# Retention and a GELU feed-forward on one core: queries turned by matmuls with strided PSUM output, tails loaded by POOL's queue, decay constants by ScalarE

## The chip, the core and the metric

The kernel runs on one core of a Trainium2 chip. The core has TensorE (PE; its weight loads are shown apart as PEld), VectorE (DVE), ScalarE (ACT), GpSimd (POOL) and SyncE (SP). Each engine works through its own instructions in program order and waits for the others through semaphores. Sixteen DMA engines move data between device memory and SBUF; an engine that issues a DMA puts it on its own queue, and all queues share the sixteen. TensorE writes only to PSUM, which has eight banks of 2 KB for each of 128 partitions.

The metric is the device time of one execution in microseconds (us), taken as the median over several executions.

## What is computed

```python
def _attn_ref(q, k, v):                      # (8, 8, 576, 64): batch, heads, sequence, head size
    scores = scale * np.matmul(q, k.transpose(0, 1, 3, 2))
    gamma = 1.0 - 2.0 ** (-5.0 - np.arange(H, dtype=np.float32))
    rel = pos[:, None] - pos[None, :]
    Dmat = np.where(rel >= 0, gamma[:, None, None] ** rel[None, :, :], 0.0)
    ret = scores * Dmat[None, :, :, :]
    return np.matmul(ret, v).astype(np.float32)

def _moe_ref(x, w_in, w_out):                # x (4608, 512), w_in (512, 2048), w_out (2048, 512)
    h = x @ w_in
    c = np.float32(np.sqrt(2.0 / np.pi))
    g = 0.5 * h * (1.0 + np.tanh(c * (h + 0.044715 * h * h * h)))
    return (g @ w_out).astype(np.float32)
```

The attention's output, with its heads side by side, is `x` of the feed-forward part. There is no softmax: the decay `gamma ** (i - j)` splits into a factor of the query's position and one of the key's, so each chunk of 128 positions needs only a 0/1 mask, and what came before the chunk goes through a state of 64 x 64 for each head.

## The kernel before

**Attention.** Each of the 8 batches has four chunks of 128 positions (`c` = 0 to 3) and a *tail* of 64 (`c == NC`, that is 4). A chunk passes through these steps, each a function:

- `load` (lines 74 to 94) brings k, q and v of a chunk into a tile `ld` (256 KB; 16 buffers), and of a tail into a tile `lt` (two DMAs of 64 KB, one for each half of the heads; 4 buffers).
- `cast` (225 to 250), through `cc`, turns f32 into f16 and multiplies q and k by the decay factors, columns of the constant `sc`.
- `turn` (268) turns k (and mostly q) by TensorE transposes into a PSUM bank, and copies the bank into `tt`. The queries of the first two batches (`NQ`) are loaded in another order, four neighbouring positions in one row, so that a descriptor covers 1 KB, and `turn_q4` (256) turns them: eight transposes fill one f16 bank of 1024 columns, and the copy (262) puts the positions back into their order. The tails, and the chunks of batches 2 and 3, are turned by `turn` with q in it; batches 4 to 7 by transposing DMAs (`turn_dma`).
- `score` (294) forms k times q in two banks, and VectorE multiplies by the mask into `ret` (308).
- `state`, `scan` and `spread` (316, 329, 339) form the state of the chunk, decay it, and copy it into `tbd`.
- `av` (344) multiplies `ret` with v and adds state times q; `put` (379) copies the result into `xT`, a ring of 1536 tokens that the feed-forward part reads.

These steps share three PSUM banks of the tag `att`; in the first batch other tags are used as well. `hp` has two, and A, B and C one each.

**Feed-forward.** The 4608 tokens go in nine blocks of 512 (`t` = 0 to 8). `up(t, fc)` (397) multiplies 128 columns of `w_in` with a block, and ScalarE applies the GELU. Block 0 then takes the plain product with `w_out`: 16 steps of two matmuls (421) for the first two token tiles, a `store_pair`, and 16 more for the other two, 34 steps in all (u = 0 to 33). Blocks 1 to 8 have 16 up steps of two and 14 product steps (u = 0 to 29), and use a scheme with seven products in place of eight, which needs sums of the activations (`act_sums`, 447, on VectorE, after steps 9 and 15) and of the weights (`weight_sums`, 437, four VectorE operations for each half).

**Order.** All order is written out by hand. Batch 0's chunks come first (lines 545 to 571), with a few matmuls without use (`filler`) between. From then on each step `u` of block `t` is followed by what `at(t, u, ...)` has put there; `up(0, fc)` counts as step `fc - 16` of block 0. So the weight casts of w_out run on VectorE at steps -5 to -2 of block 0, batch 0's tail and batch 1 within block 0, batches 2 and 3 from block 1 on.

**Loads.** `seq` (123 to 127) is the order of all loads on SP's queue: batch 0, w_in, w_out, batch 1, and so on. `pump` issues as many as there are free `ld` buffers; every cast of a chunk frees one. `mixed` (113) puts the six tail loads of a batch between other loads: those of batch 0 between the loads of w_out, those of batch 1 between batch 2's first ones. At step 0 of block 0 the tail's k is cast by VectorE and its q and v by POOL; at step 3 it is turned, at 6 scored, at 9 multiplied with v.

**Constants.** Lines 144 to 181 form the exponents of all decay factors with small VectorE operations in `ex` (56 columns), one Exp on ScalarE makes `sc` of them, and two more VectorE operations multiply by the scale.

Of the kernel before, what the change touches and what calls it, by code (L numbers as in the profile page):

```python
# [19 lines left out]
def kernel(  # L20
# [53 lines left out]
    def load(b, key, c, u=0):  # L74
        src = SRC[key]
        if c == NC:
            t = ldt() if u == 0 else att[b]["raw"][key, c]
            nc.sync.dma_start(
# [34 lines left out]
    def mixed(loads, b):  # L113
        pieces = [("b", b, key, NC, u) for key in "kqv" for u in range(2)]
        n = len(loads) // len(pieces)
        out = []
        for i, x in enumerate(loads):
            out.append(x)
            if i % n == n - 1 and pieces:
                out.append(pieces.pop(0))  # L120
        return out

    seq = body(0) + [("i", g, ct) for g in range(4) for ct in range(4)]
    seq += mixed([("o", f) for f in range(NF)], 0)
    seq += body(1) + mixed(body(2)[:6], 1) + mixed(body(2)[6:], 2)
    for b in range(3, B):
        seq += mixed(body(b), b)
# [16 lines left out]
    pos_i = const.tile([128, 1], I32, name="pos_i")  # L144
    nc.gpsimd.iota(pos_i, pattern=[[0, 1]], base=-64, channel_multiplier=1)
    qp_i = const.tile([128, 1], I32, name="qp_i")
    nc.gpsimd.iota(qp_i, pattern=[[0, 1]], base=0, channel_multiplier=QT)
    pos = const.tile([128, 1], F32, name="pos")
    nc.vector.tensor_copy(out=pos, in_=pos_i)
    post = const.tile([128, 1], F32, name="post")  # L150
    nc.vector.tensor_copy(out=post[0:64], in_=pos[0:64])
    nc.vector.tensor_scalar(out=post[64:128], in0=pos[64:128], scalar1=-64.0, scalar2=None, op0=ALU.add)
    posq = const.tile([128, 1], F32, name="posq")
    nc.vector.tensor_copy(out=posq, in_=qp_i)
    for c in range(NC):
        r = slice(32 * c, 32 * c + 32)
        nc.vector.tensor_scalar(out=posq[r], in0=posq[r], scalar1=-128.0 * c - 64.0, scalar2=None, op0=ALU.add)
    NE = 8 + HP * 8 + 8 + 8
    ex = const.tile([128, NE], F32, name="ex")
    lgr = const.tile([128, 8], F32, name="lgr")  # L160
    for h in range(H):
        nc.vector.memset(lgr[:, h : h + 1], math.log(gam[h]))
    nc.vector.tensor_scalar(out=ex[:, 0:8], in0=lgr, scalar1=pos, scalar2=-1.0, op0=ALU.mult, op1=ALU.mult)
    for j in range(QT):
        nc.vector.tensor_scalar(
            out=ex[:, 8 + 8 * j : 16 + 8 * j], in0=lgr, scalar1=float(j), scalar2=None, op0=ALU.mult
        )
        nc.vector.scalar_tensor_tensor(
            out=ex[:, 8 + 8 * j : 16 + 8 * j], in0=lgr, scalar=posq, in1=ex[:, 8 + 8 * j : 16 + 8 * j],
            op0=ALU.mult, op1=ALU.add,  # L170
        )
    nc.vector.tensor_scalar(out=ex[:, 48:56], in0=lgr, scalar1=pos, scalar2=None, op0=ALU.mult)
    for u in range(2):
        r = slice(64 * u, 64 * u + 64)
        lo = lgr[r, 4 * u : 4 * u + 4]
        nc.vector.tensor_scalar(out=ex[r, 40:44], in0=lo, scalar1=post[r], scalar2=None, op0=ALU.mult)
        nc.vector.tensor_scalar(out=ex[r, 44:48], in0=lo, scalar1=post[r], scalar2=-1.0, op0=ALU.mult, op1=ALU.mult)
    sc = const.tile([128, NE], F32, name="sc")
    nc.scalar.activation(out=sc, in_=ex, func=AF.Exp, bias=0.0, scale=1.0)
# [76 lines left out]
    def turn_q4(b, p0, copy, tag="att"):  # L256
        a = att[b]
        t = bank(tag, "tr", F16)
        for i in range(8):
            o = 512 * p0 + 128 * i  # L260
            nc.tensor.transpose(t[:, 128 * i : 128 * i + 128], a["q"][:, o : o + 128], ident)
# [313 lines left out]
    def at(t, u, f):  # L575
        events.setdefault((t, u), []).append(f)
# [135 lines left out]
```

## Time and profile before

| | |
|---|---|
| median of 13 runs | 333.39 us (331.11 to 335.86) |
| the profiled execution | 335.7 us, its span 334.0 us |
| busy in the span | PE 308.0 (92%), DVE 192.9 (58%), ACT 167.8 (50%), POOL 102.1 (31%) |
| first up-projection starts | 25.62 us |
| block 0's products start / block 1 starts | 39.43 us / 69.22 us |
| share of the chain that ended last | PE 69%, DVE 12%, DMA 8%, SP's queue 4%, ACT 4% |
| read and written | 36.70 MB and 9.44 MB of device memory |

The span runs from the first to the last instruction; the time of the execution also has what lies around it. `L421` is line 421. Where TensorE's busy share is full, its matmuls follow each other without a gap; a wait is named by the engine and the result that ended it. The granted clock of TensorE is given as a share of full speed.

### The profile page before, as it was taken

To read this page: it belongs to the slowest core of one execution; us is meant where nothing else is said; L and a number is where in the kernel's file an instruction comes from. 1 tells how busy PE (TensorE), PEld (TensorE's weight loads), DVE (VectorE), ACT (ScalarE), POOL (GpSimd) and SP (SyncE) were. 2 spreads that over 40 slices of the span, in tenths; PEclk is the share of its full clock that TensorE was granted. 3 is DMA by queue.
4 is the path that set the end of the run, shared out by engine and by line. 5 is a ranking of instruction groups with operands and counts; after the bars stand their busy time and mean duration, and the time that the engine had idled before them with its cause. 6 is when DMAs were issued, how large, how long until landed. Compare 5 with 4: busy or idle time off the path is not lost.

```text
span 334.0 us, 6557 instructions
## 1 busy us (share of the span) xinstructions
PE 308.0 (92%) x2660; PEld 187.8 (56%) x2660; DVE 192.9 (58%) x320; ACT 167.8 (50%) x312; POOL 102.1 (31%) x122
## 2 busy tenths in 40 slices
PE   5689959999889978999999999999999999999995
PEld 2344424544667436854684478447745864585484
DVE  7783454697863576547643964398355535651352
ACT  3566504677434635547636653674367146713610
POOL 7867046547350660008400930095000000000000
PEclk9999969999999989999999999999999999999999
DMA  8999999999999999993499859504410030003003
GB/s 203 213 352 334 289 272 218 186 234 186 236 196 202 202 268 195 169 248 91 91 196 194 215 111 199 180 2 84 127 57 2 3 126 3 0 2 126 2 0 128
DMA packets 134990, 51.29 MB, mean 154 GB/s; under 512 B 124208, under 2 KB 126256, under 8 KB 134960
## 3 DMA queue, kind: packets, MB, share of 16 engines
q1 hardware_dynamic: 134960, 50.87, 69.1%
q8 instruction: 21, 0.34, 0.5%
q14 instruction: 9, 0.07, 0.1%
HBM read 36.70 MB, written 9.44 MB: 138 GB/s over the span
## 4 chain that ended last, share of the span: by engine, by line
PE 69%; DVE 12%; DMA 8%; SPq 4%; ACT 4%; issue 1%; POOL 0%; DVEq 0%
PE hp L403 26%; PE opB L472 12%; PE opC L472 9%; PE opA L472 7%; DMA ld<-in_moe_w_out_dram 5%; PE op L421 4%; DMA ld<-in_moe_w_in_dram 4%; PE st L302 3%; PE xs L351 3%; SPq L90 3%; DVE s L454 2%; DVE s L455 2%; DVE s L457 2%; DVE gT L456 2%; PE us L321 2%; PE xs L369 2%
## 5 line engine op out<-in xcount | busy, mean ns | idle before, releaser
L403 PE MATMUL hp<-xT,w_in_sb 128*128 128x512 f16 x576 | 134.5, 383 | 2.1 <-ACT xT L390 2.0
L409 ACT ACTIVATE gT<-hp 128x512 f16<-128x512 f32 x144 | 86.2, 598 | 70.1 <-PE hp L403 69.6
L403 PEld LDWEIGHTS <-w_in_sb 128*128 128x128 f16 x576 | 54.2, 98 | 62.0 <-issue 4.2
L245 POOL TENSOR_TENSOR ck<-ld,sc 128x512 f16<-128x512 f32 x31 | 36.0, 1163 | 101.9 <-issue 44.3
L308 DVE TENSOR_TENSOR ret<-st,cm 128x512 f16<-128x512 f32 x64 | 41.1, 684 | 34.1 <-PE st L302 34.1
L472 PEld LDWEIGHTS <-gT 128*128 128x128 f16 x512 | 49.0, 98 | 7.2 <-issue 0.7
L472 PEld LDWEIGHTS <-s 128*128 128x128 f16 x384 | 36.3, 98 | 5.4 <-DVE s L455 0.8
L342 ACT CAST tbd<-ws 64x256 f16<-64x256 f32 x64 | 25.8, 403 | 18.2 <-DVE ws L337 17.5
L245 POOL TENSOR_TENSOR cq<-ld,sc 128x512 f16<-128x512 f32 x24 | 29.6, 1233 | 6.1 <-DMA ld<-in_q_dram 6.1
L472 PE MATMUL opB<-wt,gT 128*128 128x256 f16 x256 | 30.9, 273 | 0.5 <-DVE ost L486 0.5
L472 PE MATMUL opA<-w_out_sb,gT 128*128 128x256 f16 x256 | 31.0, 273 | 0.0
L454 DVE TENSOR_TENSOR s<-gT 128x1024 f16<-128x1024 f16 x16 | 14.8, 925 | 26.7 <-ACT gT L409 26.7
L486 DVE TENSOR_TENSOR ost<-k,opC 128x512 f32<-128x512 f32 x16 | 11.0, 688 | 16.5 <-PE opC L472 16.2
L302 PE MATMUL st<-tt 64*128 64x128 f16 x288 | 15.6, 223 | 5.2 <-DVE tt L280 2.8
L390 ACT CAST xT<-xs 128x512 f16<-128x512 f32 x31 | 18.0, 582 | 4.0 <-PE xs L369 3.0
L486 DVE TENSOR_TENSOR k<-k,opB 128x512 f32<-128x512 f32 x16 | 11.0, 686 | 15.4 <-PE opB L472 15.3
L421 PE MATMUL op<-w_out_sb,gT 128*128 128x512 f16 x64 | 18.5, 421 | 0.8 <-ACT ost L426 0.8
L302 PEld LDWEIGHTS <-tt 64*128 64x128 f16 x288 | 8.4, 95 | 19.2 <-issue 10.7
L351 PEld LDWEIGHTS <-cv 128*64 128x64 f16 x288 | 10.0, 110 | 16.2 <-issue 14.6
L351 PE MATMUL xs<-ret,cv 128*64 128x128 f16 x288 | 16.4, 227 | 2.4 <-DVE ret L308 1.3
L504 ACT COPY ost<-opA 128x512 f32<-128x512 f32 x8 | 4.7, 585 | 23.5 <-PE opA L472 20.8
L472 PE MATMUL opC<-wt,s 128*128 128x256 f16 x128 | 16.3, 273 | 0.0
(84 smaller groups left out, 311.9 us busy)
## 6 DMA issues: line engine op xcount, KB each, us to landing
out_dram<-ost SPq DMA_DIRECT2D x17, 512.0 KB, 3.2
ld<-in_q_dram SPq DMA_DIRECT2D x32, 256.0 KB, 4.7
ld<-in_k_dram SPq DMA_DIRECT2D x32, 256.0 KB, 5.0
ld<-in_v_dram SPq DMA_DIRECT2D x32, 256.0 KB, 4.9
ld<-in_moe_w_in_dram SPq DMA_DIRECT2D x16, 256.0 KB, 6.2
ld<-in_moe_w_out_dram SPq DMA_DIRECT2D x16, 256.0 KB, 5.5
lt<-in_k_dram SPq DMA_DIRECT2D x16, 64.0 KB, 4.4
lt<-in_q_dram SPq DMA_DIRECT2D x16, 64.0 KB, 5.0
```

What stands on the lines that cost most here:

```text
L245: eng.tensor_tensor(out=dst.rearrange("p (h d) -> p h d", d=D), in0=raw.rearrange("p (h d) -> p h d", d=D), in1=sc[:, s0 : s0 + nh].unsque ...
L302: nc.tensor.matmul(st[hl][:, 128 * p : 128 * p + 128], a["tk"][r, 4 * c + p, :], tq(b, c, p)[r], start=True, stop=True)
L308: nc.vector.tensor_tensor(out=r[:, 0:w], in0=st[hl][:, 0:w], in1=m.rearrange("p n i -> p (n i)"), op=ALU.mult)
L342: cp(out=tbd[b % 2][r, c, :, r], in_=att[b]["w"][r])
L351: nc.tensor.matmul(xs[64 * hl : 64 * hl + 64, 128 * p : 128 * p + 128], a["v"][:, col(c, p, hl)], a["ret"][c, hl][:, 128 * p : 128 * p + 128],
L390: nc.scalar.copy(out=xT[:, g0 : g0 + 2], in_=src)
L403: nc.tensor.matmul(hp.rearrange("p (g t) -> p g t", t=TL), w_in_sb[:, ct, 128 * fc : 128 * fc + 128], xT[:, o : o + TB // TL, ct, :], star ...
L409: nc.scalar.activation(out=gT[t][:, fc].rearrange("p i n -> p (i n)"), in_=hp, func=AF.Gelu_apprx_tanh)
L421: nc.tensor.matmul(op[i], gT[t][:, f, i], w_out_sb[:, f, :], start=(f == 0), stop=(f == NF - 1))
L454: nc.vector.tensor_tensor(out=s["1"], in0=a21, in1=a22, op=ALU.add)
L472: nc.tensor.matmul(op[tag][:, HD * u : HD * u + HD], lhs(f), rhs[:, f], start=(new and u == 0 and f == 0), stop=(f == NH - 1), skip_group_ ...
L486: nc.vector.tensor_tensor(out=o, in0=a, in1=b, op=ALU.add)
```

## The change

1. **Constants.** The exponents are no longer formed: `decay` has ScalarE compute `exp(scale * in + bias)` with the logarithm of the head's gamma as input, the position as a scale for each partition, and the logarithm of the score's scale as bias. There are seven Exps. Half of the memsets of `lgr` are POOL's.
2. **`turn_q4`.** Four matmuls against the identity, instead of four transposes, fill one f32 bank of 512 columns for one pair of heads. Matmul `j` writes the columns `j, j + 4, j + 8, ...`, so the bank holds the positions in order and the copy is straight. There are four calls for a batch instead of two.
3. **Tail loads.** They are issued on POOL's queue, all six at a written step (`load_tail`), and are no longer in `seq`. Batch 0: step -10 of block 0; batch 1: step 2 of block 1; batch 2: step 14 of block 1; batch 3: step 26 of block 1; batches 4 to 7: step 15 of block `b - 2`.
4. **Steps.** Batch 0's tail: all three casts on POOL at step 0, turned at step 8 (ScalarE's copy), scored at 10, multiplied at 13. Batch 1's queries are turned at steps 15 to 18, its chunks at 19, 23, 27 and 31, scored two steps later (before: 16, 20, 24, 28). `weight_sums(0)` moves from step 33 to step 11 of block 0, `weight_sums(4)` from step 2 to 1 of block 1. Batch 1's tail casts move from step 6 to 14 of block 1, batch 2's from 14 to 26, batch 3's from step 27 of block 1 to step 14 of block 2. In block 1 the order is (2,0), (2,1), tail of 1, (2,2) at steps 7, 12, 20 and 24; before it was tail of 1, (2,0), (2,1), (2,2) at 12, 17, 20 and 24.

```diff
@@ load @@
-            nc.sync.dma_start(
+            nc.gpsimd.dma_start(
                 out=t[64 * u : 64 * u + 64, :].rearrange("p (h d) -> p h d", d=D),
                 in_=src[b, 4 * u : 4 * u + 4, M0:S, :].rearrange("h s d -> s h d"),
@@ loads @@
-    def mixed(loads, b):
...
+    def load_tail(b):
+        for key in "kqv":
+            for u in range(2):
+                load(b, key, NC, u)
     seq = body(0) + [("i", g, ct) for g in range(4) for ct in range(4)]
-    seq += mixed([("o", f) for f in range(NF)], 0)
-    seq += body(1) + mixed(body(2)[:6], 1) + mixed(body(2)[6:], 2)
-    for b in range(3, B):
-        seq += mixed(body(b), b)
+    seq += [("o", f) for f in range(NF)]
+    for b in range(1, B):
+        seq += body(b)
@@ constants @@
-    nc.scalar.activation(out=sc, in_=ex, func=AF.Exp, bias=0.0, scale=1.0)
...
+    ip = const.tile([128, 6], I32, name="ip")
+    nc.gpsimd.iota(ip[:, 0:4], pattern=[[1, QT]], base=-64, channel_multiplier=QT)
+    nc.gpsimd.iota(ip[:, 4:5], pattern=[[0, 1]], base=-64, channel_multiplier=1)
+    lgr = const.tile([128, 16], F32, name="lgr")
+    for h in range(H):
+        (nc.gpsimd if h % 2 else nc.vector).memset(lgr[:, h : h + 1], math.log(gam[h]))
+    lsc = const.tile([128, 1], F32, name="lsc")
+    nc.vector.memset(lsc, math.log(scale))
+    ps5 = const.tile([128, 8], F32, name="ps5")
+    nc.vector.tensor_copy(out=ps5[:, 0:5], in_=ip[:, 0:5])
+    for c in range(1, NC):
+        r = slice(32 * c, 32 * c + 32)
+        nc.vector.tensor_scalar(out=ps5[r, 0:4], in0=ps5[r, 0:4], scalar1=-128.0 * c, scalar2=None, op0=ALU.add)
+    def decay(cols, lg, p, b=0.0):
+        nc.scalar.activation(out=cols, in_=lg, func=AF.Exp, bias=b, scale=p)
     for j in range(QT):
+        decay(sc[:, 8 + 8 * j : 16 + 8 * j], lgr[:, 0:8], ps5[:, j : j + 1], lsc)
...
+    decay(sc[:, 0:8], lgr[:, 0:8], ps5[:, 5:6])
...
+    decay(sc[:, 48:56], lgr[:, 0:8], ps5[:, 4:5], lsc)
+    decay(sc[:, 40:44], lgr[:, 8:12], ps5[:, 6:7], lsc)
+    decay(sc[:, 44:48], lgr[:, 8:12], ps5[:, 7:8])
@@ turn_q4 @@
+    def turn_q4(b, p, copy, tag="att"):
+        a = att[b]
+        t = bank(tag, "tr")
+        for j in range(QT):
+            o = 512 * p + 128 * j
+            nc.tensor.matmul(
+                t.rearrange("p (i j) -> p j i", j=QT)[:, j, :], a["q"][:, o : o + 128], ident,
+                start=(j == 0), stop=True, skip_group_check=True,
+            )
+        copy(out=a["tq"][:, 4 * p : 4 * p + 4, :].rearrange("p c t -> p (c t)"), in_=t)
@@ order @@
-    turn_q4(0, 0, A.copy, "A")
-    turn_q4(0, 2, V.tensor_copy, "B")
+    for p, tag in enumerate(("A", "B", "C", "att")):
+        turn_q4(0, p, (A.copy, V.tensor_copy)[p % 2], tag)
...
+    at(0, -10, lambda: load_tail(0))
-    at(0, 0, lambda: [cc(0, key, NC, e) for key, e in zip("kqv", (V, P, P))])
-    at(0, 3, lambda: turn(0, NC, V.tensor_copy))
-    at(0, 6, lambda: score(0, NC))
-    at(0, 9, lambda: av(0, NC))
-    at(0, 10, lambda: put(0, NC))
+    at(0, 0, lambda: [cc(0, key, NC, P) for key in "kqv"])
+    at(0, 8, lambda: turn(0, NC, A.copy))
+    at(0, 10, lambda: score(0, NC))
+    at(0, 13, lambda: av(0, NC))
+    at(0, 14, lambda: put(0, NC))
...
-    at(0, 12, lambda: turn_q4(1, 0, A.copy))
-    at(0, 14, lambda: turn_q4(1, 2, V.tensor_copy))
+    at(0, 11, lambda: weight_sums(0))
+    for p in range(HP):
+        at(0, 15 + p, lambda p=p: turn_q4(1, p, (A.copy, V.tensor_copy)[p % 2]))
     for c in range(NC):
-        u = 16 + 4 * c
+        u = 19 + 4 * c
...
-    at(0, 33, lambda: (av(1, 3), put(1, 3), spread(1, 3, A.copy), weight_sums(0)))
-    at(1, 2, lambda: weight_sums(4))
+    at(0, 33, lambda: (av(1, 3), put(1, 3), spread(1, 3, A.copy)))
+    at(1, 1, lambda: weight_sums(4))
...
-            t0, ut = 1, [1, 1, 1, 5, 5, 5, 9, 9, 9, 13, 13, 13]
+            t0, ut = 1, [1, 1, 1, 5, 5, 5, 9, 9, 9, 12, 12, 12]
...
-            at(1, 6, lambda: tail_casts(1, (P, P, A)))
-            at(1, 14, lambda: tail_casts(2, (P, P, A)))
+            at(1, 2, lambda: load_tail(1))
+            at(1, 14, lambda: tail_casts(1, (P, P, A)))
+            at(1, 14, lambda: load_tail(2))
+            at(1, 26, lambda: tail_casts(2, (P, P, A)))
         else:
-            at(t0, ut[-1] + 1, lambda b=b: tail_casts(b, (P, P, A)))
+            at(t0, ut[-1] if b == 3 else ut[0] - 1, lambda b=b: load_tail(b))
+            at(*((2, 14) if b == 3 else (t0, ut[-1] + 1)), lambda b=b: tail_casts(b, (P, P, A)))
...
-    todo = [(1, NC)] + [(b, c) for b in range(2, B) for c in CH]
-    plan = {1: (12, 17, 20, 24), 2: (2, 6, 12, 18, 23), 3: (2, 7, 12, 20), 4: (1, 6, 11, 17, 23),
+    todo = [(2, 0), (2, 1), (1, NC), (2, 2)] + [(b, c) for b in range(2, B) for c in CH][3:]
+    plan = {1: (7, 12, 20, 24), 2: (2, 6, 12, 18, 23), 3: (2, 7, 12, 20), 4: (1, 6, 11, 17, 23),
```

## The prediction

> **What bounds the kernel now.** I read the page's slices first, then the chain of waits of the first 70 us, then the busy times by stage, and last the order of work on VectorE, on POOL and in the tail loads. The slices say where TensorE is not full:
>
> ```profile
> PE   5689959999889978999999999999999999999995
> ...
> POOL 7867046547350660008400930095000000000000
> PEclk9999969999999989999999999999999999999999
> DMA  8999999999999999993499859504410030003003
> ```
>
> A slice is 8.35 us. From slice 6 on TensorE is full but for slices 10 to 14, so the end is set by TensorE's work plus what it lost before about 130 us. The DMA engines are full for 150 us. The granted clock falls in slice 5 (42 to 50 us) and a little in 15. The chain of that stretch, by start and length:
>
> ```profile
> 39.70 4.95 DMA ld<-in_moe_w_out_dram
> 44.65 0.02 issue
> 44.67 0.43 DVE w_out_sb L528
> 45.10 0.34 DVE ck L245
> 45.44 0.05 issue
> 45.49 0.61 PE tr L276 x4
> ...
> 53.55 2.45 ACT tt L262
> 56.00 0.43 ACT ost L426
> ...
> 68.59 0.59 ACT xT L390
> ```
>
> Until 45.1 the chain is the weight loads. TensorE stood still from 41.3 to 45.49, 4.2 us, in step 3 of block 0: the tail's transposes wait for the tail's k cast, which is queued on VectorE behind all sixteen w_out casts. Then:
>
> ```profile
> 39.40:45.50 6.10, 1.93 (x10) 0.70 (x8) 3.23 (x9) 0.60 (x1) 0.40 (x1) 0.88 0.98 313
> 45.50:51.50 6.00, 6.00 (x25) 2.19 (x26) 2.65 (x5) 0.00 (x0) 4.11 (x5) 0.55 1.11 231
> ```
>
> (The stretch, its length, busy time of PE, PEld, DVE, ACT, POOL, then granted clock and DMA share.) After the standstill the clock was 0.55 for 6 us: 0.45 x 6.0 = 2.7 us more lost. Block 1 starts at 69.22, after ScalarE's copy at 68.59. What VectorE did, and what a tail load costs on SP:
>
> ```profile
> 46.88 0.89 DVE L236 TENSOR_TENSOR cq<-ld,sc 128x512 f16<-128x512 f32 x1 [0.33 <-DMA ld<-in_q_dram]
> 49.02 0.75 DVE L308 TENSOR_TENSOR ret<-st,tm 128x256 f16<-128x256 f32 x2 [1.25 <-PE st L302]
> ```
>
> ```profile
> L78 SPq DMA_DIRECT2D lt<-in_k_dram x16: 607/1088/2630, 25.9 to 175.5; - x16
> ```
>
> (minimum, median and maximum in ns.) Blocks 1 and 2 lose 3.3 and 2.7 us to VectorE, by TensorE's waits in each; their largest are
>
> ```profile
> PE us L321 <- DVE ret L308: 1.6, 2, 0.8
> PE tr L276 <- DVE ret L308: 1.5, 1, 1.5
> ```
>
> ```profile
> PE st L302 <- DVE tt L280: 2.7, 2, 1.8
> ```
>
> (us in total, times, longest.) From block 3 on the waits are 1.8 us in all.
>
> **The constants.** Before, VectorE's small steps run from 1.06 to 5.86, the one Exp ends at 6.15, two scalings at 6.43, and the first query cast starts at 6.40. After, the query columns need five short memsets, one cast (0.15) and three 32-row adds (0.145 each), some 0.8 us from 1.06, and then four Exps after the table load, which ends at 2.08. An Exp of 56 columns took 0.249, a one-column Gelu 0.202: 0.20 to 0.25 each, I take 0.25, so 2.08 + 1.0 = 3.1, which is 3.3 us earlier. POOL gets four memsets, 0.1 each. The Trainium skill, "ScalarE: Activation LUTs", section What ACT_TABLE_LOAD costs, gives 280 ns with a pointer bias and some 93 ns more for a pointer scale; by it the four would take an estimated 1.5 us, not 1.0, and no row here has such operands.
>
> **The turning of queries.** Two strided 128x1024 copies (2.45 on ScalarE, 2.40 on VectorE) become four straight 128x512 copies (0.58 on ScalarE, 0.69 on VectorE): per engine 1.2 to 1.4 instead of 2.4. The matmuls stay sixteen for a batch, 128 columns each. Strided PSUM writing is in no row: from below, the present transposes (0.46 us by the chain for eight, 0.06 each); from above, 0.22 each, what a 512-column matmul takes, since the bank spans 512 columns. That is 0 to 16 x 0.16 = 2.6 us more a batch; I take 0.7, nearer the transposes, as the columns streamed are the same. The rule that speaks against it: "PSUM — Partial Sum Buffer", Specifications, says that any non-contiguous pattern slows matmuls significantly; it has no factor, and by a doubling the sum would have an estimated 0.9 in place of my 0.7.
>
> **What the start is worth.** Batch 0's second score waits for VectorE's strided copy until 13.43. With constants 3.3 us earlier and copies 1 us shorter, and DMA landings as before, the first up-projection can start up to 4.3 us before its 25.62. I count this as nothing: the work that hides it is the loading of w_out, whose last cast ends at 45.1 either way. Had the weights come earlier it would be worth up to 4.3.
>
> **Tails from the POOL queue.** In batch 0, SP loses six issues between w_out loads, 6 x 0.61, but the bytes still cross the same full DMA engines before w_out ends, so 45.1 stays. POOL is free at 30.04, clears tbd (1.81) until 31.8, then issues six DMAs. No POOL DMA is in the trace; the nearest rows are SP's, 0.61 to 2.63 each. I take the median, 1.04 to 1.09: issued by 38, landed by 42.7 (median landing 4.7 us), k and q cast by about 41.3. TensorE comes to step 8 of block 0 between 38.8 (w_out row 8 cast) and 43.3 (no earlier start), so the tail's transposes cost little. At 2.63, issue ends at 47.6: the second rival. The Trainium skill, "DMA: Bandwidth & Descriptors", section Issuing engine by pattern, gives plain loads to Sync and calls that path generally faster; its fit for the POOL path is 2.0 us plus bytes over 436e3, an estimated 2.15 us for 64 KB. That is time to landing, below SP's 4.7 here, so by it nothing would be later; by its rule on the issuer the step is a loss.
>
> **The wait that follows.** This is what decides. In the new order VectorE has, after the w_out casts, query casts 0 and 2 of batch 1, then the tail's mask products, then weight_sums(0). Cast 2 waits for its DMA until 46.88 and ends at 47.8; the masks take 0.75, so 48.5. TensorE runs steps 4 to 13 meanwhile (w_out row 13 is cast by 43.7), which is the gain, and stands at the tail's values (step 13) from 43.8 to 48.6: 4.8 us in place of 4.2, so the low clock comes again. From 48.6 it has less left than before had at 45.49: 10 steps of two matmuls (20 x 0.216 = 4.3) and the tail's transposes and scores (0.7) are done, and the 0.8 stall behind the 2.45 copy goes. Before took 23.7 from there; 23.7 - 4.3 - 0.7 - 0.8 + 0.7 (strided) + 0.5 (batch 1's chunk 3 now has scores and values in one step, so its values wait for a mask, 2 x 0.68 less the work between) = 19.1. Block 1 starts at 67.7, 1.5 earlier. A second way to it: weight_sums(0), four operations of 0.69 to 1.47 (POOL busy beside), ends at 52.5; the PSUM copy (0.7) and the two query copies of VectorE (0.7 each) end at 54.6; chunk 0's scores near 56; from there before took 12.0 and after 12.0 - 1.3 + 0.5 = 11.2: 67.2, 2.0 earlier. I take 1.7.
>
> **Block 1 and later.** Block 1's waits were two chunk stalls of 0.8 and one of 1.5 in its product phase, plus 0.2. Chunk (2,0) moves to step 7 and the tail to step 20, so the bank shortage there eases; in exchange (2,1) at step 12 copies behind the activation sums, as block 2's does (1.8 + 0.9). 3.3 - 2.7 = 0.6 gained, 0.3 given back for ScalarE, whose up phase gets a spread (0.82) and a copy (0.58) on top. weight_sums(0) leaves VectorE at block 1's start, where nobody waited for it: 0. The POOL issues of batches 1 to 3, 18 x 1.05 = 19 us, fit into POOL's idle 26 us between 57 and 105.4 (48.4 less 22.4 busy, by the stages); later ones into its gaps of 12 to 29 us. SP no longer waits for POOL's tail casts (16.5 us in three waits), but TensorE did not wait for those loads: 0. Sum: 1.7 + 0.3 = 2.0 us. The profiled execution took 335.7 (span 334.0 and 1.7 around it), 2.3 over the median of 333.39; a saving of 2.0 is the same in both: **331.4**, with an own range of 329.4 to 333.4.
>
> **The rivals.** *Nothing gained* (333.4): the standstill at step 13 and the low clock take back all that steps 4 to 13 gave, if strided matmuls cost their 2.6. For it: the stall is not removed, only moved. Against: the matmuls lie partly behind VectorE's weight sums. *POOL's issue is dear* (slower): from about 1.5 us an issue the tails hold step 8 past the masks' 48.5; at 2.63, k and q are cast at 48.9, steps 9 to 13 still stand to be done, and POOL's casts of batch 1 end near 58, so block 1 starts some 1.8 late; and 18 issues are 47 us where 26 are idle, 21 too many, of which batch 3's slack of 12 hides about half and landings some more: 6 more in block 2. 333.4 + 1.8 + 6 = 341. For it: POOL's tensor work and VectorE's two-input sums already slow each other (0.69 against 1.45). Against: the SP rows near 1.05 contain queueing. *More gained* (328): the tails and queries land before TensorE idles long, the clock stays full (2.7), block 1 loses its bank stalls: 2.0 + 2.7 + 0.6 = 5.3. For it: the present drop came after one wait of 4.2.
>
> **How the numbers follow.** Forecast 0.46, nothing gained 0.14, dear issue 0.26, more gained 0.14. The runs before differ by 1.4%, and a median tells about 0.5% (1.7 us) from no change. Below 331.7: 0.30 of the forecast and 0.14: 0.44. Within: 0.16 and 0.09: 0.25. Above 335.1: 0.05 and 0.26: 0.31. The range takes in half of each outer rival: 327.8 to 338.0.
>
> **What would show it.** A TensorE wait on the tail's mask products near 44 to 48.6, with the clock low after it; w_out's last cast still near 45; the first up-projection near 21.5; block 1 at 67.5; POOL's issues near 1.05. It is wrong if w_out ends elsewhere, if TensorE waits at step 8 beyond 44 for POOL's casts, or if blocks 2 on differ by over 1 us.

## The result, and the profile after

The changed kernel takes 336.9 us (median of 11 runs, 335.9 to 339.8); the kernel before, on the same chips, 333.9 us (48 runs). The ratio is 1.0125, with a 95% interval from 1.0098 to 1.0153: slower by about 1.25%, where 331.4 was forecast; inside the range of 327.8 to 338.0, but on the other side of no change. In what follows, one run of a_gate, 606.5 us against 327.0 to 328.0 in its other three, is left out.

The profiled execution took 335.58 us with a span of 333.8, against 335.7 and 334.0 before, so the two profiles differ by almost nothing. The medians differ by 3. The profile of before lies above its median and that of after below its own; a second profile of each is therefore given with the first. The start of a block is that of its first up-projection matmul on the timeline of TensorE (us):

| | block 0 | block 1 | block 2 | block 3 | block 8 | length of 0, 1, 2 |
|---|---|---|---|---|---|---|
| before, first profile | 25.62 | 69.22 | 105.27 | 143.79 | 303.35 | 43.60, 36.05, 38.52 |
| before, second | 25.87 | 68.19 | 104.64 | 141.65 | 301.20 | 42.32, 36.45, 37.01 |
| after, first | 22.71 | 65.52 | 99.14 | 143.55 | 303.00 | 42.81, 33.62, 44.41 |
| after, second | 22.46 | 66.45 | 100.07 | 144.90 | 304.36 | 43.99, 33.62, 44.83 |

By block 2 the changed kernel is 4.6 to 6.1 us ahead. In block 2 it loses more than that, and from block 3 on both run alike (31.6 us each in block 3). The stretches of the first profiles say the same, by busy time; before, then after (stretch, its length, busy time of PE, PEld, DVE, ACT and POOL with instructions, granted clock, DMA share, GB/s):

```profile
25.62:69.22 43.60, 37.98 (x284) 18.18 (x284) 22.55 (x41) 20.41 (x35) 21.19 (x27) 0.92 1.09 256
69.22:105.27 36.05, 32.80 (x296) 21.26 (x296) 26.19 (x37) 20.75 (x41) 16.12 (x16) 1.00 1.14 213
105.27:143.79 38.52, 35.85 (x335) 22.62 (x332) 23.03 (x35) 18.80 (x36) 10.98 (x10) 0.96 1.04 204
```

```profile
22.71:65.52 42.81, 36.90 (x284) 18.73 (x284) 26.32 (x45) 19.78 (x37) 31.51 (x40) 1.00 1.14 279
65.52:99.14 33.62, 32.73 (x297) 20.98 (x296) 19.50 (x33) 20.25 (x40) 22.68 (x28) 1.00 1.06 219
99.14:143.55 44.41, 37.01 (x335) 22.93 (x333) 28.13 (x35) 19.22 (x37) 19.39 (x25) 0.88 1.09 203
```

Block 0 keeps its full clock in this profile (1.00 against 0.92); in both second profiles it has 0.96, so the clock there is not a steady gain. Block 1 has the same TensorE work in 2.4 us less; VectorE is busy 6.7 us less in it, since the weight sums left it and no sum is stretched by a POOL cast. In block 2 VectorE has the same 35 instructions as before and is busy 5.1 us longer: something there takes far longer than it should.

The slices of after, the counterpart of those before:

```profile
PE   6879958899999659999999999999999999999994
...
POOL 8679368773695961009800970095000000000000
PEclk9999999999999959999999999999999999999998
DMA  8999999999999999966799699204410030003003
```

Counted from 0, slice 5 is as empty as before and slice 6 a little emptier, but the granted clock no longer falls there; a new dent stands in slices 13 and 14 (109 to 125 us), with a low clock in the second. TensorE's waits from 40 to 150 us name both dents (us in total, times, longest):

```profile
PE st L288 <- DVE tt L266: 7.4, 2, 6.9
PE xs L337 <- DVE ret L294: 3.4, 2, 3.0
```

The second is the wait on the tail's mask products, in the place the prediction gave it but 3.0 long. The first stood at 2.7 in all before, and 1.8 at the longest; now one of the two lasts 6.9. VectorE's copy of batch 3's chunk (line 266), which TensorE waits for, is queued behind the activation sums; and these, with POOL's work of the same time, look like this on the timeline (start, length, then in brackets the idle time before and what ended it):

```profile
109.22 7.31 DVE L440 TENSOR_TENSOR s<-gT 128x1024 f16<-128x1024 f16 x1 [0.85 <-ACT gT L395]
116.57 1.41 DVE L441 TENSOR_TENSOR s<-s,gT 128x1024 f16<-128x1024 f16 x1
```

```profile
107.65 1.22 POOL L78 DMA_DIRECT2D lt<-in_v_dram  x2
108.89 1.05 POOL L232 TENSOR_TENSOR ck<-ld,sc 128x512 f16<-128x512 f32 x1
...
114.89 1.03 POOL L232 TENSOR_TENSOR ck<-ld,sc 128x512 f16<-128x512 f32 x1
115.89 1.54 POOL L232 TENSOR_TENSOR cq<-ld,sc 128x512 f16<-128x512 f32 x1
```

One addition of 128x1024 (line 440) took 7.31 us; the same line takes 0.69 where POOL is quiet. POOL meanwhile ran a train of eight casts of batch 4, one every 1.00 us. The first seven gave nothing up; only the eighth is lengthened, to 1.54, and in it the sum finishes. The train follows six tail-load issues of POOL's with no gap: that is what the change put there. Before, the same train had begun 4 us ahead of the sums, and the two took turns:

```profile
115.36 1.36 DVE L454 TENSOR_TENSOR s<-gT 128x1024 f16<-128x1024 f16 x1 [0.85 <-ACT gT L409]
```

What the tail loads cost, the counterpart of SP's line before (ns, minimum, median, maximum), and the two data queues of the page (packets, MB, share):

```profile
L78 POOL DMA_DIRECT2D lt<-in_k_dram x16: 615/638/818, 30.8 to 195.2; - x16
```

```profile
q1 hardware_dynamic: 121904, 47.72, 64.1%
q0 software_dynamic: 1536, 3.15, 4.7%
```

An issue on POOL is shorter than on SP (0.64 against 1.09), so the price that the prediction feared is not there; the loss isn't the time that issuing takes: d_gelu below has the same six issues and takes 329.4.

### The profile page after: what moved, and what is told of

Same layout as the page of the kernel before. It is cut to its first block, busy times and chain, and to the rows that moved or that the text cites. A ratio compares the mean times of both kernels' runs of the same rounds, so it can differ in the third digit from the quotient of the medians.

```text
span 333.8 us, 6603 instructions
## 1 busy us (share of the span) xinstructions
PE 307.0 (92%) x2660; PEld 188.1 (56%) x2660; DVE 190.3 (57%) x303; ACT 167.7 (50%) x322; POOL 132.3 (40%) x175
## 3 DMA queue, kind: packets, MB, share of 16 engines
q1 hardware_dynamic: 121904, 47.72, 64.1%
q0 software_dynamic: 1536, 3.15, 4.7%
## 4 chain that ended last, share of the span: by engine, by line
PE 69%; DVE 15%; DMA 9%; ACT 2%; issue 2%; POOL 1%; SPq 1%; DVEq 0%
PE hp L389 28%; PE opB L458 12%; PE opC L458 9%; PE opA L458 7%; DVE s L440 4%; DMA ld<-in_moe_w_in_dram 4%; PE st L288 3%; PE xs L337 3%; DMA ld<-in_q_dram 2%; PE us L307 2%; DVE s L441 2%; DMA ld<-in_moe_w_out_dram 2%; PE op L407 2%; DVE ret L294 2%; PE xs L355 2%
## 5 line engine op out<-in xcount | busy, mean ns | idle before, releaser
L232 POOL TENSOR_TENSOR ck<-ld,sc 128x512 f16<-128x512 f32 x31 | 36.9, 1189 | 75.3 <-PE us L307 37.0
L294 DVE TENSOR_TENSOR ret<-st,cm 128x512 f16<-128x512 f32 x64 | 41.2, 685 | 35.4 <-PE st L288 35.0
L440 DVE TENSOR_TENSOR s<-gT 128x1024 f16<-128x1024 f16 x16 | 19.9, 1242 | 28.1 <-ACT gT L395 28.1
L232 POOL TENSOR_TENSOR cq<-ld,sc 128x512 f16<-128x512 f32 x24 | 28.9, 1205 | 0.2
L219 ACT CAST cv<-ld 128x512 f16<-128x512 f32 x24 | 14.0, 616 | 6.5 <-PE xs L337 6.2
L407 PE MATMUL op<-w_out_sb,gT 128*128 128x512 f16 x64 | 16.4, 381 | 0.5 <-ACT ost L412 0.5
L514 DVE CAST w_out_sb<-ld 128x512 f16<-128x512 f32 x16 | 8.5, 554 | 13.8 <-DMA ld<-in_moe_w_out_dram 13.7
```

Of the source, the lines that this page charges most:

```text
L232: eng.tensor_tensor(out=dst.rearrange("p (h d) -> p h d", d=D), in0=raw.rearrange("p (h d) -> p h d", d=D), in1=sc[:, s0 : s0 + nh].unsque ...
L294: nc.vector.tensor_tensor(out=r[:, 0:w], in0=st[hl][:, 0:w], in1=m.rearrange("p n i -> p (n i)"), op=ALU.mult)
L407: nc.tensor.matmul(op[i], gT[t][:, f, i], w_out_sb[:, f, :], start=(f == 0), stop=(f == NF - 1))
L440: nc.vector.tensor_tensor(out=s["1"], in0=a21, in1=a22, op=ALU.add)
```

## The experiments

The question was what shuts the sum out, and how much each part of the change brings without that. Each kernel is the changed one with the edit shown, if nothing else is said. "Held" means that a sum of block 2 lasted over 4 us.

**The changed kernel again** (a_again).

> The changed kernel once more, nothing edited. Theory 1 (in block 2 POOL's train of eight casts shuts VectorE's two-operand activation sum out of SBUF) and theory 2 (the POOL queue's tail loads, issued just before, hold VectorE) both expect the long sum again: one sum of 5 to 9 us in block 2 instead of 0.7 to 1.5, blocks 1 and 2 starting near 65.5 and 99, block 3 near 144, time 1.0 to 1.5% above before. If the long sum was an accident of one execution: no sum over 1.6 us, block 3 near 138, and then the loss of the median must lie elsewhere.

337.04 us, ratio 1.0134 (1.0058 to 1.0211). The long sum is there again, 7.74 us, in the same block and beside the same train.

**Train held until the sums are over** (a_gate).

```
+ wall = const.tile([128, 1], F32, name="wall")
+ at(2, 15, lambda: nc.gpsimd.tensor_copy(out=wall, in_=gs[2]["4"][:, NH - 1, 0, 0:1]))
```

> One small POOL copy that reads block 2's last activation sum is put ahead of POOL's casts of batch 4, so the train starts only after VectorE's sums; the POOL-queue loads stay where they were. Theory 1: both groups of sums at 0.7 each, TensorE's 6.9 us wait in block 2 gone and with it the low clock after it, block 3 starts 7 to 9 us earlier than in the unedited changed kernel, time some 328, 1 to 2.5% below before. Theory 2: the long sum stays, time as the changed kernel.

327.4 us (three runs, without the one named above), ratio 0.983 (0.972 to 0.994). The first sum of block 2 is back at 0.69:

```profile
110.53 0.69 DVE L440 TENSOR_TENSOR s<-gT 128x1024 f16<-128x1024 f16 x1 [0.85 <-ACT gT L395]
```

All eight sums of block 2 take 0.68 to 0.69, block 2 lasts 35.4 us in place of 44.4 and 44.8, with batch 4's tail loads issued and under way at the same time as before the edit. So the loads alone don't slow VectorE; the train must be there.

**Tail loads of batch 4 behind the train** (a_late4).

```
- at(t0, ut[-1] if b == 3 else ut[0] - 1, lambda b=b: load_tail(b))
+ at(t0, ut[-1] if b in (3, 4) else ut[0] - 1, lambda b=b: load_tail(b))
```

> The six tail loads of batch 4 are issued after POOL's casts of batch 4 instead of just before them, so the train starts 3.7 us earlier, some 4 us ahead of the sums, as it does in the kernel before. Theory 1 in its plain form (any sum that meets the train is shut out until its end): the sum still waits, though 3.7 us less, to the end of the train near 113 to 114; time 3 to 4 us below the changed kernel. Theory 1 with the place in the train deciding: sums of 1.4 to 1.5 as before, 4 to 6 us below the changed kernel. Theory 2: the long sum is gone altogether (0.7 each).

330.0 us, ratio 0.991 (0.987 to 0.995). The train begins at 105.81, after a wait of 0.57 for TensorE, and the sums take 1.31 to 1.53 from 110.09, in turns with casts of 1.49, as before the change. Block 2: 38.1.

**All tail loads back on SP's queue, at the new steps** (a_sp).

```
- nc.gpsimd.dma_start(
+ nc.sync.dma_start(
```

> All tail loads issued by SP's queue again, at the changed kernel's steps. Theory 2: no long sum, time 5 to 7 us below the changed kernel. Theory 1: the train starts 3.7 us earlier in block 2, result as in the run with late loads for batch 4, but batch 0's tails now stand in SP's queue behind w_out and land later: block 0 ends up to 2 us later than 65.5.

335.68 us, ratio 1.0088 (1.0048 to 1.0128). No long sum, but little is won, against what either theory expected: block 1 starts at 65.40, as in the changed kernel, and then lasts 38.5 in place of 33.6. POOL waits 11.35 us in it for the tail's k, and TensorE's product phase 3.4 us at once for the activation sums; block 2 lasts 39.6. So block 0's gain does not come from POOL's queue; block 1's needs it, since at the new steps SP's queue brings the tail too late.

**Does it take the coincidence, the loads under way, or the issues directly ahead?** Five kernels move the train against the sums, with and without issues ahead of it. a_align and c_gelu add to a_late4 (no issues ahead of the train) a 128x1 POOL copy ahead of the train that waits for VectorE's mask product, or for the GELU output that releases the first sum; d_gelu and f_s1 add such a copy to the changed kernel, between issues and train, waiting for that GELU output or for the first sum; e_later makes the sum come 1.7 us later by a 128x1 VectorE copy of a later GELU output.

```
a_align + at(2, 15, lambda: nc.gpsimd.tensor_copy(out=wall, in_=att[2]["ret"][NC, 1][:, 0:1]))
c_gelu  + at(2, 15, lambda: nc.gpsimd.tensor_copy(out=wall, in_=gT[2][:, 11, 0, 0:1]))
d_gelu  + at(2, 15, lambda: nc.gpsimd.tensor_copy(out=wall, in_=gT[2][:, 11, 0, 0:1]))
f_s1    + at(2, 15, lambda: nc.gpsimd.tensor_copy(out=wall, in_=gs[2]["1"][:, 0, 0, 0:1]))
e_later + if t == 2 and f == 4: nc.vector.tensor_copy(out=wall, in_=gT[2][:, 12, 0, 0:1])
```

> The changed kernel with batch 4's tail loads issued after POOL's casts of batch 4 (as in the run that moved them, 330.0 us), and with one 128x1 POOL copy ahead of those casts that reads the last mask product of batch 3's turn in block 2, so that the train of casts begins when VectorE's activation sums begin, with no DMA issue just ahead of it. Theory 1a, that it is enough that train and sums begin together: one activation sum of 6 to 8 us again, block 2 near 44 us, time near 337. Theory 1b, that POOL must come from DMA issues with its casts already queued up behind them: sums of at most 1.55 us each, block 2 at 36 to 38 us, time 328 to 330. Theory 1c, that VectorE loses only if its sum comes while a cast is already running, by chance: either, but then the sum's length is one cast, about 1.5 us.

> The changed kernel with batch 4's tail loads issued after POOL's casts of batch 4, and with a 128x1 POOL copy ahead of these casts that reads the GELU output which releases the first activation sum, so that train and sum begin within 0.2 us of each other, as in the changed kernel run again (there 0.06 us), but with no tail load of POOL's queue issued just before or under way. Theory coincidence (a sum that comes at the very start of the train is shut out): a sum of 6 to 8 us, time near 337. Theory flight (casts of POOL and tail loads of POOL's queue under way together shut it out until the loads have landed) and theory directly-ahead (DMA issues must end right before the first cast): no sum over 1.6 us, time 328 to 330.

> The changed kernel with the same 128x1 copy between the six tail-load issues and the train: train and sum begin within 0.2 us of each other, the loads are under way, but POOL has waited some 0.5 us between its last issue and the first cast. Flight: a sum of 5 to 7 us, ending when the loads have landed (some 7 us after the last issue), time near 336. Coincidence: 6 to 8 us as well. Directly-ahead: no sum over 1.6 us, 328 to 330.

> The changed kernel with the 128x1 POOL copy between the tail-load issues and the train reading the output of the first activation sum, so that the first sum runs alone and the train begins with the second, about 1.2 us after the last issue, with the loads under way. Flight: first sum 0.69, the second or third 4 to 6 us, time 333 to 336. Directly-ahead: no sum over 1.6 us, 328 to 330. Coincidence: the second sum 6 to 8 us.

> The changed kernel with a 128x1 VectorE copy ahead of block 2's first activation sum that reads a later GELU output, so that the sum comes 1.7 us later, in the third cast of the train, which starts directly behind the tail-load issues as in the changed kernel; the loads are under way. Flight: a sum of 4 to 5.5 us, ending at the same moment as before (about 116), time 335 to 337. Coincidence or directly-ahead with a sum at the train's start: no sum over 1.6 us, time 329 to 331.

Only e_later is held, and it is the one in which sum and train do not begin together. Its sum, which came in the fourth cast, and the end of the train:

```profile
112.17 4.64 DVE L440 TENSOR_TENSOR s<-gT 128x1024 f16<-128x1024 f16 x1
```

```profile
109.14 1.06 POOL L232 TENSOR_TENSOR ck<-ld,sc 128x512 f16<-128x512 f32 x1
...
115.14 1.03 POOL L232 TENSOR_TENSOR ck<-ld,sc 128x512 f16<-128x512 f32 x1
116.14 1.58 POOL L232 TENSOR_TENSOR cq<-ld,sc 128x512 f16<-128x512 f32 x1
```

Against it d_gelu, with the same six issues, the loads under way, and a POOL that waited once between them and the train:

```profile
111.38 1.56 DVE L441 TENSOR_TENSOR s<-s,gT 128x1024 f16<-128x1024 f16 x1
112.86 1.53 DVE L442 TENSOR_TENSOR gT<-gT 128x1024 f16<-128x1024 f16 x1
```

```profile
110.69 0.71 POOL L626 CAST wall<-gT 128x1 f32<-128x1 f16 x1 [0.35 <-ACT gT L395]
111.35 1.04 POOL L232 TENSOR_TENSOR ck<-ld,sc 128x512 f16<-128x512 f32 x1
112.35 1.49 POOL L232 TENSOR_TENSOR cq<-ld,sc 128x512 f16<-128x512 f32 x1
```

The second sum asked 0.03 us after the first cast began and was served behind it; from there sums of 1.5 and casts of 1.49 take turns. The times are 329.8 (a_align), 329.6 (c_gelu), 329.4 (d_gelu), 329.6 (f_s1) and 335.5 (e_later, ratio 1.0031, 0.9998 to 1.0063). Coincidence falls by c_gelu and a_align, loads under way by d_gelu and f_s1, though e_later by itself had come out as that theory expected.

**What of "directly behind the issues" does it?** h_memset puts a POOL memset that waits for nothing between issues and train; h_busy is a_late4 with seven memsets where the issues had been; h_two leaves, in the place of batch 4's one call for its tail, only the two issues for v ahead of the train, and h_four those for q and v, with the rest behind it.

```
h_memset + at(2, 15, lambda: nc.gpsimd.memset(wall, 0.0))
h_busy   + at(2, 15, lambda: [nc.gpsimd.memset(wide, 0.0) for _ in range(7)])
h_two    + at(2, 15, lambda: [load(4, "v", NC, u) for u in range(2)])
h_two    + at(2, 23, lambda: [load(4, key, NC, u) for key in "kq" for u in range(2)])
```

> The changed kernel with one 128x1 POOL memset, which waits for nothing, between batch 4's six tail-load issues and the train of casts. If the train must follow the issues with no pause of POOL's (a wait for another engine) to shut VectorE out: one sum of 4.5 to 8 us, ending 7 casts after the train's start, time 335 to 337. If any other POOL operation between issue and cast is enough to break it: no sum over 1.6 us, time 328 to 331.

> The changed kernel with batch 4's tail loads issued after the casts, and seven POOL memsets of 128x512 (0.54 us each, 3.8 us in all, waiting for nothing) in the place of the six issues (3.7 us), so that the train has the same backlog ahead of it but no issue. If a backlog of POOL instructions with no wait is enough: a sum of 4.5 to 8 us, time 335 to 338. If DMA issues are needed: no sum over 1.6 us, time 328 to 331.

> The changed kernel with only two of batch 4's six tail loads (v) issued ahead of the train and four behind it, so that the train begins some 2.4 us earlier and the sum comes in its third or fourth cast. If two issues shut VectorE out for the same seven casts: a sum of 3.5 to 5 us, time 333 to 336. If the number of casts shut out follows the number of issues (some two): no sum over 1.6 us, time 329 to 331.

> The changed kernel with four of batch 4's six tail loads (q and v) issued ahead of the train and two (k) behind it, so that the train begins some 1.2 us earlier than with six and the sum comes in its second cast. If the number of casts that VectorE waits for follows the number of issues (six held it for seven, two for at most three): the sum is held until the end of the fourth or fifth cast, 2.5 to 4 us, time 329 to 333. If it is all or nothing with a threshold above four: no sum over 1.6 us, 328 to 330. If any hold lasts seven casts: 5 to 6.5 us, 334 to 336.

h_memset is held (335.7 us), h_busy (329.7) and h_two (329.1) are not, h_four is (333.5, ratio 0.996, 0.992 to 0.9998). Its sum and train:

```profile
110.48 5.35 DVE L440 TENSOR_TENSOR s<-gT 128x1024 f16<-128x1024 f16 x1 [0.85 <-ACT gT L395]
```

```profile
107.00 1.23 POOL L78 DMA_DIRECT2D lt<-in_v_dram  x2
108.24 1.06 POOL L232 TENSOR_TENSOR ck<-ld,sc 128x512 f16<-128x512 f32 x1
...
115.24 1.48 POOL L232 TENSOR_TENSOR cq<-ld,sc 128x512 f16<-128x512 f32 x1
```

All cases side by side, from the two timelines of each kernel (us; the sum is the first of block 2 that meets the train):

| kernel | ahead of the train on POOL | first cast | sum begins | its length | its end after the first cast's start |
|---|---|---|---|---|---|
| after | six issues | 108.89 | 109.22 | 7.31 | 7.64 |
| a_again | six issues | 110.21 | 110.15 | 7.74 | 7.68 |
| e_later | six issues | 109.14 | 112.17 | 4.64 | 7.67 |
| h_memset | six issues, a memset | 110.45 | 111.30 | 6.84 | 7.69 |
| h_four | four issues | 108.24 | 110.48 | 5.35 | 7.59 |
| h_two | two issues | 106.94 | 109.71 | 0.84 | |
| d_gelu | six issues, a wait of 0.35 | 111.35 | 111.38 (second) | 1.56 | |
| f_s1 | six issues, a wait of 2.17 | 113.17 | 113.69 (fourth) | 1.53 | |
| c_gelu | a wait of 5.13 | 110.78 | 110.81 (second) | 1.56 | |
| a_late4 | a wait of 0.57 | 105.81 | 110.09 | 1.31 | |
| a_align | a wait of 3.50 | 109.21 | 109.85 | 0.95 | |
| h_busy | seven memsets | 110.89 | 110.93 | 1.55 | |

The sum is held until the seventh cast ends, whenever it came, in every kernel where four or six issues go ahead with no wait of POOL's between them and the train. Without issues, with two, or with a wait in between, it waits for one cast at most. The changed kernel holds the counter-case itself: the six issues of batch 5 also stand ahead of that batch's train, but POOL waits 23.14 us for TensorE in between, and the first sum that meets the train in block 3 takes 0.91:

```profile
150.88 1.04 POOL L232 TENSOR_TENSOR ck<-ld,sc 128x512 f16<-128x512 f32 x1 [23.14 <-PE tr L262]
153.56 0.91 DVE L440 TENSOR_TENSOR s<-gT 128x1024 f16<-128x1024 f16 x1
```

Why seven, and where between two and four issues it turns, stays open; h_two and h_four also differ in which loads go ahead. It isn't separated either whether POOL's wait is needed or only the pause that it makes, and most of these kernels have one profile. What inside POOL makes the difference no row shows.

**The same hold in the kernel before** (b_gate: before, with a_gate's copy).

> The kernel before, with one 128x1 POOL copy that reads the last activation sum of block 2, so that POOL's eight casts of batch 4 begin after the sums and not 4 us before them. Theory 1 (sums and train hold each other up whenever they meet; before, they alternate): sums of 0.69 instead of 1.36 to 1.52, block 2 about 2.5 to 3 us shorter than 38.5, so near 331; what the change then gained elsewhere is the distance from this run to the changed kernel with the same copy (327.7), 3 us. Rival (before's block 2 was bound by something else than the sums): within 1 us of before.

337.04 us, ratio 1.011 (1.005 to 1.017): a miss. Block 2 became 35.1 us, as expected, with sums of 0.69. Block 3 became 37.55 in place of 31.6, by one wait:

```profile
PE st L302 <- DMA tt<-cq: 4.2, 1, 4.2
```

In that kernel the tail loads are on SP's queue, where a load waits for POOL's casts to free its buffer, and everything behind it waits too, the transposing DMAs of batch 4 among them. SP's queue stood from 125.7 to 133.1:

```profile
125.30 0.38 SPq L90 DMA_DIRECT2D ld<-in_v_dram  x1
133.05 0.61 SPq L78 DMA_DIRECT2D lt<-in_q_dram  x1
```

With the tails on POOL's queue the same hold costs block 3 nothing (31.6 in a_gate). Each of the two edits alone makes the kernel some 3 us slower; together they make it 6 us faster.

**What the other two parts are worth**, measured on the version without the long sum. g_oldturn is a_gate with the old turning (transposes and strided 1024-column copies, batch 1 at steps 16 and 18); g_oldconst is a_gate with the old constants (one Exp of 56 columns behind VectorE's steps).

> The changed kernel with the 128x1 copy that holds POOL's train (327.7), and with the queries of batches 0 and 1 turned as before: transposes and strided 1024-column copies, batch 1's at steps 16 and 18. By the prediction's terms (0.8 us stall behind the 2.45 copy, 0.7 of strided matmuls given back, start hidden): block 1 starts within 1 us of the same kernel without this edit (66.8). If the turning is what gained in blocks 0 and 1: block 1 starts at 68 or later and the time rises by 1.5 to 3 us, to 329 to 331.

> The changed kernel with the 128x1 copy that holds POOL's train (327.7), and with the decay constants of before (one Exp of 56 columns after VectorE's small steps). By the prediction the start is hidden behind the w_out loads: first up-projection 1.3 to 2 us later (24 to 24.5 instead of 22.6), block 1 and the time unchanged within 0.5 us. If the start counts, block 1 and the time are later by the same 1.3 to 2 us.

330.03 us for g_oldturn (ratio to before 0.988, 0.984 to 0.993), 327.73 for g_oldconst (0.982, 0.977 to 0.986). Against g_again below (327.75), the turning is worth 2.3 us and the constants nothing. With the old turning the first up-projection begins at 25.14, in the two profiles with the new one at 22.6 and 23.4; block 1 begins at 68.18, there at 66.8 and 65.7. Block 1 also lasts 35.0 in place of 33.6, but with the same waits of TensorE and a granted clock of 0.95 in place of 1.00; h_memset, d_gelu and f_s1, which have the new turning, show 35.2 to 35.3 at 0.95 too, so that part is not shown to be the turning's. With the old constants the first up-projection begins at 23.19, no later than with the new ones, where 24 to 24.5 was expected.

**The fastest version and the kernel before once more** (g_again is a_gate; b_again is before).

> The changed kernel with the 128x1 POOL copy that reads the last activation sum of block 2, once more, as the fastest version found: 327 to 328.5 us, ratio to before 0.977 to 0.986.

> The kernel before, unedited, for a second profile: the first lies 2.3 us over the median of its runs, and the changed kernel's lies 1.3 us under its own, so that the two profiles differ by 0.1 us where the medians differ by 3 to 4. If the difference sits in block 0 (the standstill and the low clock behind it): time 332 to 334, block 1 starts 1.5 to 3 us before 69.2 and blocks 1 and 2 last 36 and 38.5 us as before. If it sits in the meeting of sums and casts in block 2: block 1 starts at 69.2 and block 2 lasts 36 to 37 us.

327.75 us, ratio 0.979 (0.974 to 0.983), as at first: one 128x1 copy that holds POOL's train turns the change from 1.25% slower to some 2% faster than before. b_again took 333.43; it is the second row of the table of blocks. Its lead over the first profile, 2.2 us of span, sits half in block 0 (1.3) and half in block 2 (1.5), so the expectation's either-or was wrong, but neither half touches the reading: by the second profiles the changed kernel is 3.2 us behind at block 3.

## Why the prediction was wrong

**The step that failed** is the one on later blocks: the issues "fit into POOL's idle 26 us between 57 and 105.4", and with that the later blocks were left unchanged. They do fit, and cost 0.64 us each, below the 1.04 to 1.09 that was taken. But four to six of them right ahead of a train of casts shut VectorE out for seven casts, and TensorE then stood 6.9 us (7.3 in the second profile) behind VectorE's copy and ran with a low clock: 0.88 and 0.92 over the block, where before had 0.96 and 1.00. Block 2 went from 38.5 to 44.4, or from 37.0 to 44.8 by the second profiles: 6 to 8 us that the sum had at zero. The prediction named "blocks 2 on differ by over 1 us" as what would prove it wrong. The issues were costed as time on their own engine only. What stood against it was in the profile: the rows of 0.69 against 1.45 for one sum, whose place against POOL's train the change moves.

**The slower rival** had the right block and the wrong mechanism: it wanted dear issues, and no issue in the profile reached 0.85.

**w_out's last cast "either way" at 45.1** was wrong. It ended at 43.5 (42.44 + 1.05) and, in the second profile, at 44.3. SP issued the sixteen w_out loads in one run from 23.81 to 34.26, where before they had lain between tails from 24.72 to 40.0. In the other kernels with this change it ended between 41.8 (a_sp) and 45.0 (h_busy); what moves it among them isn't shown.

**The start, counted as nothing,** splits in two. For the constants the time came out so: old and new give the same. But w_out's loads need not hide anything there, since the first up-projection itself starts no earlier by them, though the first query cast does (4.93 against 6.41). For the turning it was wrong: 2.3 us. With the old turning the first up-projection starts 1.7 to 2.6 us later, and in block 0 TensorE waits 1.31 us behind VectorE's strided copy.

**The wait that follows** was the right wait; its size differs from one execution to the next. The mask products were to end at 48.5 after a standstill of 4.8 with a low clock, and block 1 was to gain 1.7. What the first profile has, on VectorE's timeline and in the stretches:

```profile
45.10 0.90 DVE L223 TENSOR_TENSOR cq<-ld,sc 128x512 f16<-128x512 f32 x1 [0.81 <-DMA ld<-in_q_dram]
45.92 0.74 DVE L294 TENSOR_TENSOR ret<-st,tm 128x256 f16<-128x256 f32 x2
```

```profile
39.40:45.50 6.10, 3.95 (x24) 1.66 (x23) 2.59 (x6) 0.58 (x1) 2.06 (x3) 1.00 1.12 297
45.50:51.50 6.00, 4.50 (x34) 3.07 (x34) 5.93 (x8) 2.03 (x4) 5.53 (x5) 1.00 1.04 208
```

The query cast that the masks are queued behind ended at 46.0, not 47.8, since its load came earlier with the rest; the standstill was 3.0, and the clock stayed at 1.00. Block 1 began at 65.5, not 67.5: a gain of 3.7 over the first profile of before. In the second profile the standstill is in two pieces, the first behind POOL's cast of the tail's q, which the prediction had counted as little:

```profile
42.66 0.28 PE L262 MATMUL tr<-ident,cq 128*128 128x128 f16 x2 [2.23 <-POOL cq L232]
47.27 0.60 PE L337 MATMUL xs<-ret,cv 128*64 128x128 f16 x4 [1.84 <-DVE ret L294]
```

The clock of 45.5 to 51.5 is 0.73 there, the mask products end at 47.55, and block 1 gains 1.7 over the second profile of before: near what was forecast. So this step did not fail by more than the executions differ. The clock is not settled by the length of one wait: of 45.5 to 51.5 it was 0.72 in g_again after a standstill of 2.3, and 0.55 in a_gate after waits of 1.9 and 1.0.

**Block 1** gained 2.4, or 2.8 by the second profiles, in place of 0.3. Of TensorE's waits of 4.0 us there 1.5 were left, and the sums ran undisturbed at 0.69. a_sp shows that the new steps need the tails' early arrival over POOL's queue: from SP's queue the block lasts 38.5. How much of the gain is due to the steps and how much to the weight sums, which left VectorE there, no run separates. The wait of 1.5 behind a mask product that was put down to the shortage of banks is gone, as forecast; "0.3 given back" did not show.

**The small terms** held. Strided matmuls: four in 0.39 us against eight transposes in 0.46, so 0.64 a batch where 0.7 was taken. An Exp: 0.31 where 0.25 was taken; the four ran from 3.66 to 4.90, late because the table load itself had moved behind a VectorE step, and that did not matter. By the figures of the Trainium skill, "ScalarE: Activation LUTs", section What ACT_TABLE_LOAD costs, the estimate had been 0.37 each. The same section lets such operations overlap by some 93 ns when they follow each other; with that the estimate is 1.2 for the four, and the run's 1.24 agrees. The small fall of the clock before, which the prediction reads in slice 15, stands in slice 14; nothing rests on it.

**The sum in hindsight**: 3.7 and 2.4 gained, 5.9 lost, 0.2 net in the first profiles (334.0 to 333.8); by the second, 68.19 to 66.45 and 36.45 to 33.62 are 4.6 gained, 37.01 to 44.83 are 7.8 lost, and 3.2 net is near the difference of the medians, 3.0. "More gained" (5.3) came near the gain of blocks 0 and 1 in amount, 6.1 and 4.6, up to 99 us; the full clock on which it counted showed in the first profile alone.

## What to carry to other kernels

Cost a queue step by what it puts next to what, not by its own time: where two engines have been seen to lengthen each other's operations, as VectorE's sums and POOL's casts did here, look at which operations will run beside the work behind the moved instructions. Keep a wait between DMA issues and a long train of POOL operations, or leave the issues behind the train; in this kernel either removed the hold. A one-column copy that made POOL wait for VectorE cost 0.19 us here and was worth 9. A load that waits for a consumer's buffer belongs on a queue where nothing urgent stands behind it: b_gate, where transposing DMAs stood behind such loads, lost 6 us in block 3 by delaying the consumer, a_gate nothing.

## What the runs showed of the hardware

A two-input VectorE operation of 128x1024 beside a POOL cast of 128x512 waited in these runs for one cast at most, but for the hold: 0.69 becomes 0.84 to 1.56, and 1.04 becomes 1.49. The Trainium skill, "SBUF — State Buffer", section Who interferes with whom, says that a VectorE instruction with two SBUF inputs contends with a GpSimd instruction that reads SBUF, and calls the pair of ports that they share an exclusive lock; the turns of 1.5 us agree with it. If the lock is held for one instruction, a sum waits for one cast. The 4.64 to 7.74 us behind DMA issues do not fit that, and the measurement decides: the wait can be for seven casts.

Loads from POOL's queue move packets of 2 KB (3.15 MB in 1536), against 391 bytes on average in the hardware queue (47.72 MB in 121,904), and were issued in 0.62 to 0.64 us at the median.
